# Attention then MoE on one core: a new opening for batch 0, a new bank order in the first s1, and w_in by columns

## The chip, the cores and the metric

One NeuronCore of one Trainium2 chip runs the whole kernel. The metric is the device time of one execution in microseconds (us). The kernel before takes 332.48 us (median of 3 runs, 332.35 to 333.21). The engines are named as in the profile: PE (TensorE matmul), PEld (its weight loads), DVE (VectorE), ACT (ScalarE), POOL (GpSimd), SP (SyncE). PSUM is the memory into which PE writes its results; a bank is the piece of it that takes one 128x512 float32 result. A load "lands" when the trace reports it complete.

## The reference

```python
# q, k, v: (8 batches, 8 heads, 576 tokens, 64), float32
scores = q @ k^T / 8                       # mask: 0 <= query - key < 64
attn   = softmax(scores) ; a = attn @ v
x      = a, heads side by side             # (4608, 512)
h      = x @ w_in                          # w_in (512, 2048)
g      = h * clip(h + 3, 0, 6) / 6
out    = g @ w_out                         # w_out (2048, 512), out (4608, 512) float32
```

## The kernel before

The tokens go through the MoE in nine blocks T of 512. `s1(T)` makes 16 blocks `fc` of hidden units (four matmuls each, then ACT and DVE), `s2(T)` multiplies by `w_out`. Attention of a batch is interleaved with an earlier MoE block, but batch 0 has nothing to hide behind: its attention, then `s1(0)`, then `s2(0)` mixed with batch 1's attention are the opening of the program. This is the part that the change touches.

Loads and set-up (cut):

```python
    stage0, ins0 = load_qk_for_pe(0, 2)   # on SP: q pair 0, k pair 0, the 64-token rests of q and k,
    vst0, insv0 = load_v_by_head(0)       # then q and k of pairs 1 to 3; then V, head by head
    ...
    for i in range(NQT):                  # all rings are zeroed at once, on DVE
        for ring, n in ((QT_ring, "QT"), (KT_ring, "KT")):
            t = consts.tile([P, NG, SP], BF16, name=f"{n}{i}")
            nc.vector.memset(t[:, :, S:SP], 0.0)
    ... # four pT and two V in the same way
```

The first MoE block. Its four first banks are the halves of two `st` tiles:

```python
    def s1_bank(fc):
        if fc in (12, 13):
            return (ps_o, ps_acc)[fc - 12].tile([P, 512], F32, name=("o", "acc")[fc - 12])[:]
        if fc % 4 < 2:
            return h_bank()[:]
        return ps_st.tile([P, 2, 512], F32, name=f"st{fc % 2}")[:, 0, :] if fc < 12 else h_bank()[:]
    ...
        if first:                                    # s1(0) alone
            for u in range(2):
                t = ps_st.tile([P, 2, 512], F32, name=f"st{u}")
                banks += [t[:, 0, :], t[:, 1, :]]
            for gs in first:
                for fc in range(4):
                    mms(fc, banks[fc], gs)
                yield
        for fc in range(NFC):
            hT = banks[fc] if fc < len(banks) else s1_bank(fc)
            mms(fc, hT, (NG - 1,) if fc < len(banks) else range(NG))
            t1 = t1pool.tile([P, TB], BF16, name="t1")
            nc.scalar.activation(out=t1[:], in_=hT, func=RELU, bias=half[:], scale=1.0 / 6.0)
            nc.vector.scalar_tensor_tensor(
                out=gT[:, fc, :], in0=t1[:], scalar=1.0, in1=hT, op0=MIN, op1=MULT)
            yield
```

The weights are cast by the DMA that POOL issues, and POOL also casts q, k and V, in the order of the program:

```python
    w_in = [load_w_in(0, 512, 0, NG)]
    bt.cast_v(vst0, KB - 1, KB, 0, H, pcopy)
    bt.cast_v(vst0, 0, KB - 1, 0, 2, pcopy)
    bt.cast_v(vst0, 0, KB - 1, 2, 4, pcopy)
    w_in += [load_w_in(512, 1024, 0, NG)]
    bt.cast_v(vst0, 0, KB - 1, 4, 6, pcopy)
    bt.cast_v(vst0, 0, KB - 1, 6, 8, pcopy)
    w_in += [load_w_in(1024, FF, 0, 2), load_w_in(1024, FF, 2, NG)]
    ...
    m = s1(0, ((0, 1), (2,)))
    run(m, 1)
    X_(bt, 3)
    run(m, 1)
    st1, ins = load_qk_for_pe(1, 4)
    for x in ins:
        after(x, w_in[1], "the weights go first")
    vst1, _ = load_v_by_head(1)
    ...
    bt.cast_qk(st, 0, 0, 4, pcopy)
    load_w_out(0)
    bt.cast_qk(st, 1, 0, 4, pcopy)
    bt.cast_rest(st, pcopy)
    load_w_out(1)
    cast_pairs(bt, st, 4, 4)
    load_w_out(2)
    load_w_out(3)
    run(m, 11)
    TT(bt, 0, oa_tr)          # batch 1, pair 0: transposes of q and k
    run(m)
    ...
    m = s2(0, BY_QUARTER)     # first all that needs w_out's quarter 0, then quarter 1, ...
    RR(bt)                    # batch 1: transposes of the 64-token rest
```

The softmax here doesn't subtract the row's maximum and nothing guards it: scores larger than these inputs give would overflow.

Of the kernel before, what the change touches and what calls it, by code (L numbers as in the profile page):

```python
# [9 lines left out]
F32 = mybir.dt.float32  # L10
BF16 = mybir.dt.bfloat16
# [13 lines left out]
def kernel(  # L25
# [9 lines left out]
    nc = tc.nc  # L35
    P = nc.NUM_PARTITIONS
    B, H, S, D = q.shape
    DM, FF = moe_w_in.shape
    NT = B * S
    NG = H // 2  # L40
    assert D == 64 and NG * P == DM and WINDOW == D
    KB = (S + P - 1) // P
    SP = KB * P
    NPE = 3
    R = 4
    SM = P * R
    SR = S - SM
    NFC = FF // P
    TB = 512
# [3 lines left out]
    VW = D + 1  # L53
    scale = 1.0 / math.sqrt(D)

    consts = ctx.enter_context(tc.tile_pool(name="consts", bufs=1))
    stage = ctx.enter_context(tc.tile_pool(name="stage", bufs=1))
# [5 lines left out]
    ps_st = ctx.enter_context(tc.tile_pool(name="ps_st", bufs=1, space=PSUM))  # L63
    ps_o = ctx.enter_context(tc.tile_pool(name="ps_o", bufs=1, space=PSUM))
    ps_h = ctx.enter_context(tc.tile_pool(name="ps_h", bufs=2, space=PSUM))
    ps_acc = ctx.enter_context(tc.tile_pool(name="ps_acc", bufs=1, space=PSUM))

    def after(ins, dep, why):

        tc.add_manual_dep(  # L70
            ins.ins, dep.ins.name,
            mybir.DependencyInfo(mybir.DependencyClass.Sync, mybir.DependencyReason.DATA),
            reason=why,
        )
# [24 lines left out]
    def load_qk_for_pe(b, heads):  # L99
        qst = stage.tile([P, H, R * D], F32, name="qst", tag="qst")  # L100
        kst = stage.tile([P, H, R * D], F32, name="kst", tag="kst")
        rst = stage.tile([P, H, D], F32, name="rst", tag="rst")
        ins = []
        for h0 in range(0, H, heads):
            for dst, src in ((qst, q), (kst, k)):
                ins.append(nc.sync.dma_start(
                    out=dst[:, h0 : h0 + heads, :],
                    in_=src[b, h0 : h0 + heads, 0:SM, :].rearrange("h (p j) d -> p h (j d)", j=R),
                ))
            if h0 == 0:  # L110
                for i, src in enumerate((q, k)):
                    ins.append(nc.sync.dma_start(
                        out=rst[i * SR : (i + 1) * SR, :, :],
                        in_=src[b, :, SM:S, :].rearrange("h s d -> s h d"),
                    ))
        return (qst, kst, rst), ins

    def load_v_by_head(b):
        vst = stage.tile([P, KB, H, D], F32, name="vst", tag="vst")
        ins = load_blocks(vst, v, b, (KB - 1,)) + load_v(b, vst, 0, H)  # L120
        return vst, ins

    def load_for_dma(b):
# [5 lines left out]
        return tuple(sts), ins  # L129

    ctx.enter_context(tc.manual_schedule())
    stage0, ins0 = load_qk_for_pe(0, 2)
    vst0, insv0 = load_v_by_head(0)


    ident = consts.tile([P, P], BF16, name="ident")
    make_identity(nc, ident[:])
    mask1 = consts.tile([P, QW], BF16, name="mask1")
# [2 lines left out]
        out=mask1[:], in_=mask1[:], pattern=[[1, QW]], compare_op=ISGE,  # L141
# [3 lines left out]
        out=mask1[:], in_=mask1[:], pattern=[[-1, QW]], compare_op=ISGE,  # L145
# [16 lines left out]
    QT_ring, KT_ring, P_ring, V_ring = [], [], [], []  # L162
    for i in range(NQT):
        for ring, n in ((QT_ring, "QT"), (KT_ring, "KT")):
            t = consts.tile([P, NG, SP], BF16, name=f"{n}{i}")
            nc.vector.memset(t[:, :, S:SP], 0.0)
            ring.append(t)
    for i in range(NPT):
        t = consts.tile([P, 2, KB, 2 * P], BF16, name=f"pT{i}")
        nc.vector.memset(t[:, :, 0 : KB - 1, QW : 2 * P], 0.0)  # L170
        nc.vector.memset(t[:, :, KB - 1, P : 2 * P], 0.0)
        P_ring.append(t)
    for i in range(NV):
        t = consts.tile([P, KB, H, VW], BF16, name=f"V{i}")
        nc.vector.memset(t[:, :, :, D:VW], 1.0)
        nc.vector.memset(t[D:P, KB - 1, :, 0:D], 0.0)
        V_ring.append(t)

    mask = consts.tile([P, 2 * KB, QW], BF16, name="mask")

    win16 = consts.tile([P, NG, FF], BF16, name="win16")
    wout16 = consts.tile([P, NFC, DM], BF16, name="wout16")
    xT = consts.tile([P, NG, NT + SP - S], BF16, name="xT")

    def load_w_in(f0, f1, g0, g1):
        return nc.gpsimd.dma_start(
            out=win16[:, g0:g1, f0:f1],
            in_=moe_w_in[g0 * P : g1 * P, f0:f1].rearrange("(g p) f -> p g f", p=P),
        )
# [176 lines left out]
    def h_bank():  # L366
        return ps_h.tile([P, 512], F32, name="hT")
# [1 line left out]
    def h_tr():  # L369
        return ps_h.tile([P, 1024], BF16, name="hT")  # L370

    def s1_bank(fc):
        if fc in (12, 13):
            return (ps_o, ps_acc)[fc - 12].tile([P, 512], F32, name=("o", "acc")[fc - 12])[:]
        if fc % 4 < 2:
            return h_bank()[:]
        return ps_st.tile([P, 2, 512], F32, name=f"st{fc % 2}")[:, 0, :] if fc < 12 else h_bank()[:]
# [12 lines left out]
    def s1(T, first=()):  # L390
        t0 = T * TB
        gT = gpool.tile([P, NFC, TB], BF16, name="gT")
        gTs[T] = gT

        def mms(fc, hT, gs):
            for g in gs:
                nc.tensor.matmul(  # L397
                    hT, lhsT=win16[:, g, fc * P : (fc + 1) * P],
                    rhs=xT[:, g, t0 : t0 + TB], start=(g == 0), stop=(g == NG - 1),
                )  # L400

        banks = []
        if first:
# [5 lines that stand above are left out]
                    mms(fc, banks[fc], gs)  # L409
                yield  # L410
        for fc in range(NFC):
            hT = banks[fc] if fc < len(banks) else s1_bank(fc)
            mms(fc, hT, (NG - 1,) if fc < len(banks) else range(NG))
            t1 = t1pool.tile([P, TB], BF16, name="t1")
            nc.scalar.activation(out=t1[:], in_=hT, func=RELU, bias=half[:], scale=1.0 / 6.0)  # L415
            nc.vector.scalar_tensor_tensor(  # L416
                out=gT[:, fc, :], in0=t1[:], scalar=1.0, in1=hT, op0=MIN, op1=MULT,
            )
            yield
# [25 lines left out]
    def run(gen, n=10 ** 6):  # L445
        for _ in range(n):
            if next(gen, "end") == "end":
                break
# [21 lines left out]
    def do(bt, *key):  # L470
        later.pop((bt.b, *key))()

    def N_(bt, g, banks=None):
        n = [pv(bt, g, h, next(banks) if banks else h_bank()) for h in range(2)]
        n[0]()
        n[1]()
# [9 lines left out]
    def RR(bt, banks=None):  # L486
        R_(bt, banks)
        do(bt, "r")
# [8 lines left out]
    def cast_pairs(bt, st, h0, heads):  # L497
        bt.cast_qk(st, 0, h0, heads, pcopy)
        bt.cast_qk(st, 1, h0, heads, pcopy)


    bt, st = Batch(0), stage0
    cast_pairs(bt, st, 0, 2)
    bt.cast_rest(st, pcopy)
    for g in range(1, NG):
        cast_pairs(bt, st, 2 * g, 2)
    w_in = [load_w_in(0, 512, 0, NG)]
    bt.cast_v(vst0, KB - 1, KB, 0, H, pcopy)
    bt.cast_v(vst0, 0, KB - 1, 0, 2, pcopy)
    bt.cast_v(vst0, 0, KB - 1, 2, 4, pcopy)  # L510
    w_in += [load_w_in(512, 1024, 0, NG)]
    bt.cast_v(vst0, 0, KB - 1, 4, 6, pcopy)
    bt.cast_v(vst0, 0, KB - 1, 6, 8, pcopy)
    w_in += [load_w_in(1024, FF, 0, 2), load_w_in(1024, FF, 2, NG)]

    def S0_(g, u):
        later[0, "s", g, u] = scores(bt, g, u, bias=True)

    def T0_(g):
        for i in range(2):  # L520
            later[0, "qk"[i], g] = bt.main_t(g, i, h_tr(), vcopy if g else None)

    T0_(0)
    later[0, "r"] = bt.rest_t(ps_acc.tile([P, 1024], BF16, name="acc"))
    do(bt, "q", 0)
    do(bt, "k", 0)
    S0_(0, 0)
    T0_(1)
    do(bt, "r")
    do(bt, "q", 1)  # L530
    do(bt, "s", 0, 0)
    S0_(0, 1)
    do(bt, "k", 1)
    do(bt, "s", 0, 1)
    for g in range(1, NG):
        S0_(g, 0)
        if g == NG - 1:
            N_(bt, 0, oa)
        if g + 1 < NG:
            T0_(g + 1)  # L540
        S0_(g, 1)
        if g + 1 < NG:
            do(bt, "q", g + 1)
            do(bt, "k", g + 1)
        do(bt, "s", g, 0)
        do(bt, "s", g, 1)
    N_(bt, 1, oa)
    X_(bt, 0)
    N_(bt, 2, oa)
# [8 lines left out]

    st1, ins = load_qk_for_pe(1, 4)
    for x in ins:  # L560
        after(x, w_in[1], "the weights go first")
    vst1, _ = load_v_by_head(1)

    nc.vector.tensor_copy(
        out=mask[:], in_=mask1[:].unsqueeze(1).to_broadcast([P, 2 * KB, QW])
    )
# [6 lines left out]
    cast_pairs(bt, st, 4, 4)  # L573
    load_w_out(2)
    load_w_out(3)
    run(m, 11)
    TT(bt, 0, oa_tr)
    run(m)

    bt.cast_v(vst1, KB - 1, KB, 0, H, pcopy)  # L580
    for g in range(NG):
# [1 line left out]
    st2, _ = load_qk_for_pe(2, 4)  # L583

    m = s2(0, BY_QUARTER)
    RR(bt)
    T_(bt, 1)
    S_(bt, 0, 0)
    S_(bt, 0, 1)
# [114 lines left out]
```

## Time and profile before

| | before |
|---|---|
| time | 332.48 us |
| span of the profiled execution | 330.2 us |
| PE busy | 309.0 us (94%) |
| idle gaps of PE over 0.15 us, all | 15.1 us, of which 13.9 before 74 us |
| w_out's four quarters land at | 39.99, 43.38, 46.68, 50.11 us |
| they are first used at | 45.75, 48.52, 51.30, 53.84 us |

From the page, part 2: the span in 40 slices of 8.25 us, a digit being tenths of a slice.

```profile
PE   2995889989999999999999999999999999999995
PEclk9997999999999999999999999999999999999999
DMA  7999999999382999199919991999100010021011
```

PE falls under 9 only in the first nine slices and the last, and the DMA engines are full from the second slice to the tenth. So only the opening can gain, and it has two possible limits, PE's own chain and the DMA. After it, a gain is kept: PE stays fed to the end.

From the timeline of before, PE alone (us: start, length, line, output and inputs, count, and in brackets the idle time before it and what ended it):

```profile
4.28 0.61 PE L263 MATMUL hT<-ident,qn 128*128 128x128 bf16 x4 [4.28 <-POOL qn L233]
...
12.51 0.40 PE L263 MATMUL hT<-ident,qn 128*128 128x128 bf16 x4
...
26.64 0.59 PE L397 MATMUL st<-xT,win 128*128 128x512 bf16 x2 [1.50 <-DVE gT L416]
29.11 0.58 PE L397 MATMUL st<-xT,win 128*128 128x512 bf16 x1 [1.88 <-DVE gT L416]
29.49 3.32 PE L397 MATMUL hT<-xT,win 128*128 128x512 bf16 x8
...
34.38 1.89 PE L397 MATMUL hT<-xT,win 128*128 128x512 bf16 x8
...
45.75 1.04 PE L428 MATMUL o<-wout,gT 128*128 128x512 bf16 x4
...
53.13 0.78 PE L297 MATMUL st<-QT,KT 64*128 64x192 bf16 x10
53.84 1.04 PE L428 MATMUL o<-wout,gT 128*128 128x512 bf16 x4
```

Three readings. Four transposes take 0.61 us at 4 us and 0.40 us at 12.5 us: PE is at half clock at first, although PEclk shows a 9 there. In s1(0) PE waits 1.50 and 1.88 us for DVE although the bank it wants to write is not the one that DVE reads: the two banks are halves of one `st` tile, and the built program orders accesses by tile (of the two matmuls at 26.64 the first is for the other half of the tile that DVE has just read, and had to wait; the second is for the other tile, and went on without a wait). The Trainium skill ("PSUM — Partial Sum Buffer", PSUM bank collisions raise a hardware error) says that two engines must be kept apart in the same bank and quadrant, and that on different banks they run clean; so this wait is the program's, not the hardware's. The trace agrees as far as it goes: from 34.43 to 35.12 us DVE reads an st bank while PE writes hT banks. Last, eight matmuls take 3.32 us just after these waits and 1.89 us later: the clock was halved in between, after a stretch in which PE was mostly idle.

### The profile page before, as it was taken

To read this page: it belongs to the slowest core of one execution; us is meant where nothing else is said; L and a number is where in the kernel's file an instruction comes from. 1 tells how busy PE (TensorE), PEld (TensorE's weight loads), DVE (VectorE), ACT (ScalarE), POOL (GpSimd) and SP (SyncE) were. 2 spreads that over 40 slices of the span, in tenths; PEclk is the share of its full clock that TensorE was granted. 3 is DMA by queue.
4 is the path that set the end of the run, shared out by engine and by line. 5 is a ranking of instruction groups with operands and counts; after the bars stand their busy time and mean duration, and the time that the engine had idled before them with its cause. 6 is when DMAs were issued, how large, how long until landed. Compare 5 with 4: busy or idle time off the path is not lost.

```text
span 330.2 us, 5923 instructions
## 1 busy us (share of the span) xinstructions
PE 309.0 (94%) x2291; PEld 158.8 (48%) x2332; DVE 191.9 (58%) x341; ACT 200.8 (61%) x321; POOL 83.9 (25%) x112
## 2 busy tenths in 40 slices
PE   2995889989999999999999999999999999999995
PEld 1462444545555455544554455446544554444442
DVE  5564665558763777387637773878377637504700
ACT  2664767268864876488647863887378737516711
POOL 4722705533700344025402540255000000000000
PEclk9997999999999999999999999999999999999999
DMA  7999999999382999199919991999100010021011
GB/s 212 231 180 265 241 203 256 237 254 198 85 223 77 220 193 230 66 219 198 236 64 216 202 228 57 220 207 218 62 31 2 35 65 34 1 77 50 2 64 64
DMA packets 128732, 48.89 MB, mean 148 GB/s; under 512 B 114624, under 2 KB 123840, under 8 KB 128704
## 3 DMA queue, kind: packets, MB, share of 16 engines
q1 hardware_dynamic: 124672, 43.27, 60.7%
q0 software_dynamic: 4032, 5.24, 8.7%
q8 instruction: 18, 0.29, 0.4%
q14 instruction: 10, 0.08, 0.1%
HBM read 36.70 MB, written 9.44 MB: 140 GB/s over the span
## 4 chain that ended last, share of the span: by engine, by line
PE 90%; DVE 3%; ACT 2%; DMA 1%; issue 1%; SPq 0%; POOL 0%; POOLq 0%
PE o L428 19%; PE acc L428 19%; PE hT L397 19%; PE st L397 14%; PE st L297 5%; PE hT L332 3%; PE hT L358 2%; PE o L397 2%; PE acc L397 2%; PE hT L337 2%; DMA rst<-in_k_dram 1%; DVE gT L416 1%; PE st L291 1%; ACT t L415 1%; PE hT L263 1%
## 5 line engine op out<-in xcount | busy, mean ns | idle before, releaser
L397 PEld LDWEIGHTS <-win 128*128 128x128 bf16 x576 | 55.9, 98 | 71.3 <-issue 7.5
L428 PEld LDWEIGHTS <-gT 128*128 128x128 bf16 x576 | 52.5, 98 | 56.5 <-issue 0.4
L416 DVE SCALAR_TENSOR_TENSOR gT<-t,hT 128x512 bf16<-128x512 bf16 x70 | 47.6, 687 | 47.8 <-ACT t L415 47.8
L428 PE MATMUL acc<-wout,gT 128*128 128x512 bf16 x272 | 67.6, 379 | 1.2 <-issue 0.6
L428 PE MATMUL o<-wout,gT 128*128 128x512 bf16 x279 | 67.6, 379 | 1.0 <-issue 0.3
L397 PE MATMUL hT<-xT,win 128*128 128x512 bf16 x273 | 67.4, 385 | 0.4 <-issue 0.2
L306 ACT ACTIVATE pT<-st 128x768 bf16<-128x768 f32 x64 | 49.2, 809 | 12.4 <-PE st L297 12.3
L397 PE MATMUL st<-xT,win 128*128 128x512 bf16 x219 | 53.2, 380 | 3.6 <-DVE gT L416 3.4
L415 ACT ACTIVATE t<-hT,half 128x512 bf16<-128x512 f32 x70 | 47.6, 692 | 12.8 <-PE hT L397 12.6
L320 DVE TENSOR_TENSOR pT<-pT,mask 128x1920 bf16<-128x1920 bf16 x28 | 39.1, 1395 | 19.8 <-ACT pT L312 19.8
L416 DVE SCALAR_TENSOR_TENSOR gT<-t,st 128x512 bf16<-128x512 bf16 x56 | 38.4, 688 | 13.8 <-ACT t L415 13.6
L415 ACT ACTIVATE t<-st,half 128x512 bf16<-128x512 f32 x56 | 38.4, 687 | 12.0 <-PE st L397 11.3
L363 ACT COPY xT<-hT 128x576 bf16<-128x576 bf16 x32 | 20.5, 640 | 25.2 <-PE hT L358 24.8
L434 ACT COPY osb<-o 128x512 f32<-128x512 f32 x18 | 10.6, 588 | 36.6 <-PE o L428 36.6
L208 POOL CAST V<-vst 64x512 bf16<-64x512 f32 (+2 forms) x22 | 26.0, 1201 | 26.3 <-DMA vst<-in_v_dram 26.3
L213 POOL CAST qn<-qst 128x512 bf16<-128x512 f32 x20 | 11.4, 611 | 83.2 <-DMA qst<-in_q_dram 74.1
L348 DVE TENSOR_TENSOR opg<-hT,rec 128x320 bf16<-128x320 f32 x56 | 27.5, 492 | 1.9
L332 PEld LDWEIGHTS <-pT 128*128 128x128 bf16 x320 | 20.6, 97 | 8.5 <-issue 0.9
L345 DVE RECIPROCAL rec<-hT 128x5 f32<-128x5 f32 x56 | 10.6, 189 | 22.3 <-PE hT L337 22.2
L332 PE MATMUL hT<-V,pT 128*128 128x65 bf16 x280 | 19.2, 193 | 0.5 <-ACT xT L363 0.4
L297 PE MATMUL st<-QT,KT 64*128 64x192 bf16 (+1 forms) x320 | 19.2, 243 | 0.3
L434 ACT COPY osb<-acc 128x512 f32<-128x512 f32 x18 | 10.7, 592 | 14.4 <-PE acc L428 14.4
(77 smaller groups left out, 237.1 us busy)
## 6 DMA issues: line engine op xcount, KB each, us to landing
out_dram<-osb SPq DMA_DIRECT2D x32, 256.0 KB, 2.0
qst<-in_q_dram SPq DMA_DIRECT2D x24, 256.0 KB, 4.6
kst<-in_k_dram SPq DMA_DIRECT2D x24, 256.0 KB, 5.4
vst<-in_v_dram SPq DMA_DIRECT2D x20, 256.0 KB, 5.8
vst<-in_v_dram SPq DMA_DIRECT2D x32, 128.0 KB, 5.7
win<-in_moe_w_in_dram POOLq DMA_DIRECT2D x4, 512.0 KB, 6.5
qst<-in_q_dram SPq DMA_DIRECT2D x4, 512.0 KB, 7.5
kst<-in_k_dram SPq DMA_DIRECT2D x4, 512.0 KB, 8.6
```

The source lines that it names most:

```text
L208: copy(out=self.V[:kp, k0:k1, h0:h1, 0:D], in_=vst[:kp, k0:k1, h0:h1, :])
L297: nc.tensor.matmul(st[:, h, off : off + w], lhsT=bt.KT[h * D : (h + 1) * D, g, kb * P : (kb + 1) * P], rhs=bt.QT[h * D : (h + 1) * D, g, k ...
L306: nc.scalar.activation(out=pT[:, :, 2 * u : 2 * u + 2, 0:QW], in_=st[:, :, 0 : 2 * QW].rearrange("p h (k w) -> p h k w", k=2), func=EXP, s ...
L320: nc.vector.tensor_tensor(out=pT[:, :, :, 0:QW], in0=pT[:, :, :, 0:QW], in1=mask[:].rearrange("p (h k) w -> p h k w", h=2), op=MULT,)
L332: nc.tensor.matmul(ob, lhsT=pT[:, h, qb, 0:P], rhs=V[:, qb, 2 * g + h, :], start=True, stop=(qb == 0),)
L348: nc.vector.tensor_tensor(out=opgs[bt.b, g][:, :, h, :], in0=ov[:, :, 0:D], in1=rec[:].unsqueeze(2).to_broadcast([P, KB, D]), op=MULT,)
L363: return lambda: acopy(out=xT[:, g, bt.b * S : (bt.b + 1) * S], in_=tr[:, 0:S])
L397: nc.tensor.matmul(hT, lhsT=win16[:, g, fc * P : (fc + 1) * P], rhs=xT[:, g, t0 : t0 + TB], start=(g == 0), stop=(g == NG - 1),)
L415: nc.scalar.activation(out=t1[:], in_=hT, func=RELU, bias=half[:], scale=1.0 / 6.0)
L416: nc.vector.scalar_tensor_tensor(out=gT[:, fc, :], in0=t1[:], scalar=1.0, in1=hT, op0=MIN, op1=MULT,)
L428: nc.tensor.matmul(accs[ts], lhsT=gT[:, fc, ts * P : (ts + 1) * P], rhs=wout16[:, fc, :], start=(fc == 0), stop=(fc == NFC - 1),)
L434: nc.scalar.copy(out=osb[:], in_=accs[ts])
```

## The change

The intent is to shorten the opening: have k of pair 0 early (ACT's queue), put the 64-token rests and the memsets out of the way, have PE's clock up early (matmuls on zeros), let s1(0) start as four banks in twos so that PE does not alternate with DVE, bring w_in in the order in which s1(0) uses it, and finish batch 1's first transposes before s2(0). The diff, cut to its core:

```diff
-    stage0, ins0 = load_qk_for_pe(0, 2)
+    def load_first():
...
+                eng = nc.scalar if h0 == 0 and src is k else nc.sync
...
+            if h0 == 2:
+                (the rests of q and k are loaded here)
...
+    stage0, ins0 = load_first()
     vst0, insv0 = load_v_by_head(0)
+    after(insv0[0], ins0[4], "the third pair goes first")
+    xT = consts.tile([P, NG, NT + SP - S], BF16, name="xT")
+    nc.vector.memset(xT[:, 0, 0:TB], 0.0)
+    idle = ps_o.tile([P, 512], F32, name="o")
+    def keep_busy(n):
+        for _ in range(n):
+            nc.tensor.matmul(
+                idle[:], lhsT=xT[:, 0, 0:P], rhs=xT[:, 0, 0:TB], start=True, stop=True,
+            )
+    keep_busy(8)
...
     (memsets of the rings become fill_qk, fill_p, fill_v, called where they are first needed)
...
-    def s1_bank(fc):
+    def s1_bank(fc, T):
+        if T == 0:
+            if fc in (6, 7):
+                return (ps_o, ps_acc)[fc - 6].tile([P, 512], F32, name=("o", "acc")[fc - 6])[:]
+            if fc in (8, 9, 12, 13):
+                return ps_st.tile([P, 2, 512], F32, name=f"st{fc % 2}")[:, 0, :]
+            return h_bank()[:]
...
-            hT = banks[fc] if fc < len(banks) else s1_bank(fc)
-            mms(fc, hT, (NG - 1,) if fc < len(banks) else range(NG))
+            if fc < len(banks):
+                hT = banks[fc]
+                if fc % 2 == 0:
+                    mms(fc, hT, (NG - 1,))
+                    mms(fc + 1, banks[fc + 1], (NG - 1,))
+            else:
+                hT = s1_bank(fc, T)
+                mms(fc, hT, range(NG))
...
-    w_in = [load_w_in(0, 512, 0, NG)]
     bt.cast_v(vst0, KB - 1, KB, 0, H, pcopy)
     bt.cast_v(vst0, 0, KB - 1, 0, 2, pcopy)
-    bt.cast_v(vst0, 0, KB - 1, 2, 4, pcopy)
-    w_in += [load_w_in(512, 1024, 0, NG)]
-    bt.cast_v(vst0, 0, KB - 1, 4, 6, pcopy)
-    bt.cast_v(vst0, 0, KB - 1, 6, 8, pcopy)
-    w_in += [load_w_in(1024, FF, 0, 2), load_w_in(1024, FF, 2, NG)]
+    w_in = [load_w_in(0, 512, 0, NG)]
+    for h0 in (2, 4, 6):
+        bt.cast_v(vst0, 0, KB - 1, h0, h0 + 2, pcopy)
+    w_in += [load_w_in(f, f + 512, 0, NG) for f in (512, 1024, 1536)]
...
-        after(x, w_in[1], "the weights go first")
+        after(x, w_in[2], "the weights go first")
...
-    run(m, 11)
+    run(m, 15)
     TT(bt, 0, oa_tr)
     run(m)
+    RR(bt, oa_tr)
...
     m = s2(0, BY_QUARTER)
-    RR(bt)
```

More of the change, by code (lines that the diff above doesn't have):

```diff
@@ L131 @@
     ctx.enter_context(tc.manual_schedule())
-    stage0, ins0 = load_qk_for_pe(0, 2)
-    vst0, insv0 = load_v_by_head(0)
+    def load_first():
+        qst = stage.tile([P, H, R * D], F32, name="qst", tag="qst")
+        kst = stage.tile([P, H, R * D], F32, name="kst", tag="kst")
+        rst = stage.tile([P, H, D], F32, name="rst", tag="rst")
+        ins = []
+        for h0 in range(0, H, 2):
+            for dst, src in ((qst, q), (kst, k)):
+                eng = nc.scalar if h0 == 0 and src is k else nc.sync
+                ins.append(eng.dma_start(
+                    out=dst[:, h0 : h0 + 2, :],
+                    in_=src[0, h0 : h0 + 2, 0:SM, :].rearrange("h (p j) d -> p h (j d)", j=R),
+                ))
+            if h0 == 2:
+                for i, src in enumerate((q, k)):
+                    nc.sync.dma_start(
+                        out=rst[i * SR : (i + 1) * SR, :, :],
+                        in_=src[0, :, SM:S, :].rearrange("h s d -> s h d"),
+                    )
+        return (qst, kst, rst), ins
+    stage0, ins0 = load_first()
+    vst0, insv0 = load_v_by_head(0)
+    after(insv0[0], ins0[4], "the third pair goes first")
[6 more added lines that the diff above has]
+                idle[:], lhsT=xT[:, 0, 0:P], rhs=xT[:, 0, 0:TB], start=True, stop=True,
+            )
+    keep_busy(8)
     ident = consts.tile([P, P], BF16, name="ident")
@@ L164, with fill_qk, fill_p, fill_v @@
         for ring, n in ((QT_ring, "QT"), (KT_ring, "KT")):
-            t = consts.tile([P, NG, SP], BF16, name=f"{n}{i}")
-            nc.vector.memset(t[:, :, S:SP], 0.0)
-            ring.append(t)
+            ring.append(consts.tile([P, NG, SP], BF16, name=f"{n}{i}"))
     for i in range(NPT):
-        t = consts.tile([P, 2, KB, 2 * P], BF16, name=f"pT{i}")
+        P_ring.append(consts.tile([P, 2, KB, 2 * P], BF16, name=f"pT{i}"))
+    for i in range(NV):
+        V_ring.append(consts.tile([P, KB, H, VW], BF16, name=f"V{i}"))
+    def fill_qk(i):
+        for ring in (QT_ring, KT_ring):
+            nc.vector.memset(ring[i][:, :, S:SP], 0.0)
+    def fill_p(i):
+        t = P_ring[i]
         nc.vector.memset(t[:, :, 0 : KB - 1, QW : 2 * P], 0.0)
         nc.vector.memset(t[:, :, KB - 1, P : 2 * P], 0.0)
-        P_ring.append(t)
-    for i in range(NV):
-        t = consts.tile([P, KB, H, VW], BF16, name=f"V{i}")
+    def fill_v(i):
+        t = V_ring[i]
         nc.vector.memset(t[:, :, :, D:VW], 1.0)
         nc.vector.memset(t[D:P, KB - 1, :, 0:D], 0.0)
-        V_ring.append(t)
+    fill_qk(0)
+    fill_p(0)
     mask = consts.tile([P, 2 * KB, QW], BF16, name="mask")
@@ L182 @@
     wout16 = consts.tile([P, NFC, DM], BF16, name="wout16")
-    xT = consts.tile([P, NG, NT + SP - S], BF16, name="xT")
     def load_w_in(f0, f1, g0, g1):
@@ L502 @@
     bt, st = Batch(0), stage0
-    cast_pairs(bt, st, 0, 2)
-    bt.cast_rest(st, pcopy)
-    for g in range(1, NG):
+    for g in range(NG):
         cast_pairs(bt, st, 2 * g, 2)
-    w_in = [load_w_in(0, 512, 0, NG)]
+        if g == 1:
+            bt.cast_rest(st, pcopy)
     bt.cast_v(vst0, KB - 1, KB, 0, H, pcopy)
     bt.cast_v(vst0, 0, KB - 1, 0, 2, pcopy)
-    bt.cast_v(vst0, 0, KB - 1, 2, 4, pcopy)
-    w_in += [load_w_in(512, 1024, 0, NG)]
-    bt.cast_v(vst0, 0, KB - 1, 4, 6, pcopy)
-    bt.cast_v(vst0, 0, KB - 1, 6, 8, pcopy)
-    w_in += [load_w_in(1024, FF, 0, 2), load_w_in(1024, FF, 2, NG)]
+    w_in = [load_w_in(0, 512, 0, NG)]
+    for h0 in (2, 4, 6):
+        bt.cast_v(vst0, 0, KB - 1, h0, h0 + 2, pcopy)
+    w_in += [load_w_in(f, f + 512, 0, NG) for f in (512, 1024, 1536)]
     def S0_(g, u):
@@ L523 @@
     T0_(0)
-    later[0, "r"] = bt.rest_t(ps_acc.tile([P, 1024], BF16, name="acc"))
     do(bt, "q", 0)
     do(bt, "k", 0)
+    keep_busy(2)
     S0_(0, 0)
     T0_(1)
+    later[0, "r"] = bt.rest_t(ps_acc.tile([P, 1024], BF16, name="acc"))
+    do(bt, "s", 0, 0)
+    do(bt, "q", 1)
     do(bt, "r")
-    do(bt, "q", 1)
-    do(bt, "s", 0, 0)
+    do(bt, "k", 1)
     S0_(0, 1)
-    do(bt, "k", 1)
     do(bt, "s", 0, 1)
+    fill_p(1)
+    fill_v(0)
     for g in range(1, NG):
@@ L546 @@
         do(bt, "s", g, 1)
+        if g + 1 < NG:
+            fill_p(g + 1)
     N_(bt, 1, oa)
@@ L560 @@
     for x in ins:
-        after(x, w_in[1], "the weights go first")
+        after(x, w_in[2], "the weights go first")
     vst1, _ = load_v_by_head(1)
+    fill_qk(1)
+    fill_v(1)
     nc.vector.tensor_copy(
```

## The prediction

> **What bounds the kernel now.** The page: PE busy 309.0 of 330.2 us. PE idle gaps over 0.15 us (timeline) sum to about 15 us, and nearly all lie before 74 us; afterwards PE is fed, so only the opening can gain, and what it gains stays.
>
> The opening, from the timeline and from the DMA issues with their landings:
> - 0 to 22.1 us, attention of batch 0. PE waits 4.28 (q cast), 1.08 (k of pair 0, landing at 5.25 behind q) and 1.21 (rest of k, landing at 6.99). Then the exponentials pace it, 2.1 us a pair, the first at 9.51. Four transposes take 0.61 us until about 12 us and 0.40 later: the clock is cold although the record says 1.00. The Trainium skill ("TensorE: Matmul & The Clock Gate", Part 1) describes this: throttled until one window of about 3.4 us is busy.
> - 22.1 to 42.5 us, s1(0). After the first chunk PE waits 1.50 and 1.88 us for gT: the two banks of one st tile are treated as one, so matmul, ACT and DVE alternate. The idleness drops the granted clock (0.90 and 0.76 in 25:30 and 30:35), and eight matmuls take 3.32 instead of 1.89 us. The transposes of batch 1 cost a wait of 0.79.
> - 42.5 to 45.8 us: waits of 0.64, 0.48, 0.22 around the rest of batch 1.
> - The DMA is full (share about 1.0 or more) from 2 to 50 us. The quarters of w_out land at 40.0, 43.4, 46.7, 50.1 us; s2(0) first uses them at 45.8, 48.5, 51.3, 53.8. Slack of the last: only 3.7 us.
>
> **What the change does.**
> 1. K of pair 0 on ACT's queue, the rest later, memsets out of DVE's way: first exponential about 1.5 to 2 us earlier; s1(0) starts at about 20.5 instead of 22.1. The DMA work is the same (the skill, "DMA: Bandwidth & Descriptors", Issuing engines are not separate DMA queues: all queues share 16 engines), so k of pair 3 and V do not come much earlier.
> 2. Idle matmuls (8 of about 0.43 us, then 2): warm clock some 4 to 7 us earlier. PE mostly waits there, so little by itself.
> 3. Banks in twos: removes 1.50+1.88, most of the 1.4 of half clock and the 0.79; ACT and DVE then pace, 0.72 us a block. About 5 us.
> 4. Rest of batch 1 before s2: about 0.4 us.
> 5. w_in by columns: quarter 0 lands about 1 us later (20), quarters 1 to 3 in time (about 22.5, 25, 28). Batch 1's loads start near 25 instead of 22.45, yet the bytes in front are the same: they land at most 1 us earlier, and so does w_out.
>
> PE alone could reach s2(0) about 7 us sooner (near 38.5). But w_out is DMA-bound and comes only about 1 us sooner: PE will wait for w_out in s2(0), and the last quarter (about 49) fixes the gain: 53.8 - 49.2 = about 4.5 us.
>
> **Predicted: 327.8 us**, 325.5 to 330.0 eight times in ten. Faster by over 2%: 0.13; within 2%: 0.85; slower: 0.02.
>
> **Signs.** Right: first exponential at 7.5 to 8.2; s1(0) from about 20.5; no wait of over 1 us for gT; no half-clock window near 30; new PE waits for DMA w_out of 2 to 4 us in total between 38 and 50; last quarter used at about 49; after 70 us the trace is merely shifted by 4 to 5 us. Wrong: w_out landing before 47 (gain near 7), or PE waiting for w_in in s1(0).
>
> **What would make it wrong.** Batch 1's loads, gated later, landing late and delaying w_out's issue (gain under 3); new idleness bringing the half clock back; w_out's share of the DMA growing because V of batch 1 comes later (gain over 6).

## More of the kernel before

From the windows of before (stretch in us, length, busy time and count of PE, PEld, DVE, ACT, POOL, then granted clock, DMA share, GB/s moved; a share is the summed time of the packets over 16 engines, so it can exceed 1):

```profile
18.00:21.00 3.00, 2.64 (x60) 2.05 (x55) 2.79 (x9) 2.00 (x4) 1.65 (x3) 1.00 1.19 204
...
25.55:28.97 3.42, 0.59 (x2) 0.19 (x2) 1.88 (x3) 1.58 (x3) 0.00 (x0) 1.00 1.09 278
28.97:32.38 3.41, 3.27 (x8) 1.13 (x8) 0.93 (x3) 1.37 (x2) 1.72 (x2) 0.50 1.19 268
```

The last two are neighbouring stretches of 3.41 us: 0.59 us of PE work in the first, half clock in the second.

## The result, and the profile after

The changed kernel takes 329.75 us (median of 4, 329.46 to 330.45) against 332.59 for the kernel before in the same job. The ratio is 0.9915, 95% interval 0.9893 to 0.9937: a gain of about 2.8 us. A ratio here and below is the mean time of one kernel's runs over that of the other's of the same rounds, so it is not quite the ratio of the medians.

| | before | after |
|---|---|---|
| span of the profiled execution, us | 330.15 | 328.26 |
| first exponential | 9.51 | 6.92 |
| s1(0) starts | 22.08 | 20.59 |
| PE ready for s2(0) | 45.75 | 38.50 |
| s2(0) starts | 45.75 | 41.98 |
| w_in loads land | 18.84, 22.38, 25.97, 29.13 | 20.54, 23.75, 26.45, 29.85 |
| first q of batch 1 lands | 30.13 | 31.32 |
| w_out's quarters land | 39.99, 43.38, 46.68, 50.11 | 41.93, 45.32, 48.62, 52.05 |
| last quarter first used | 53.84 | 52.10 |
| from there to the end of the span | 276.31 | 276.16 |

(Landings are those that the trace gives for each DMA issue; "PE ready" is the end of PE's work before its wait. The profiled pair shows 1.9 of the 2.8 us: the profiled execution of after, 330.45 us, was the slowest of its four.)

From the page of after, part 2, the same three rows:

```profile
PE   7989589899999999999999999999999999999995
PEclk9999869999999999999999999999999999999999
DMA  8999999999983998399929992999200110021011
```

PE is busier at the start, but the half clock has moved from the fourth slice to the fifth and sixth, and PE has a new low (a 5) in the fifth, near 40 us. The timeline of PE in after shows what it is:

```profile
1.25 3.60 PE L163 MATMUL o<-xT 128*128 128x512 bf16 x8 [1.25 <-DVE xT L158]
4.89 0.52 PE L303 MATMUL hT<-ident,qn 128*128 128x128 bf16 x4
...
20.59 1.90 PE L443 MATMUL st<-xT,win 128*128 128x512 bf16 x8 [0.41 <-DMA win<-in_moe_w_in_dram]
...
24.36 1.89 PE L443 MATMUL hT<-xT,win 128*128 128x512 bf16 x8
...
29.07 1.02 PE L443 MATMUL st<-xT,win 128*128 128x512 bf16 x4 [0.24 <-DVE gT L468]
...
36.91 0.38 PE L285 MATMUL o<-ident,rn 128*128 128x128 bf16 x4 [0.79 <-DVE QT L308]
...
41.98 1.89 PE L480 MATMUL o<-wout,gT 128*128 128x512 bf16 x4 [3.48 <-DMA wout<-in_moe_w_out_dram]
43.66 1.91 PE L480 MATMUL acc<-wout,gT 128*128 128x512 bf16 x4
45.36 0.63 PE L303 MATMUL hT<-ident,qn 128*128 128x128 bf16 x4
...
51.38 0.79 PE L337 MATMUL st<-QT,KT 64*128 64x192 bf16 x10
52.10 1.04 PE L480 MATMUL o<-wout,gT 128*128 128x512 bf16 x4
```

All that the change set out to do on PE has happened: the clock is up by 5 us, the waits for gT are 0.24 us, and PE is ready for s2(0) 7.25 us sooner (38.50 against 45.75). Then it waits 3.48 us for w_out, and works at half clock when it starts again (four matmuls in 1.89 us, against 1.04 later).

That accounts for the 7.25 us: 3.48 are the wait, 2.03 are the half clock (from s2(0)'s start to the use of the last quarter PE takes 10.12 us, against 8.09 in before), and 1.74 are left as gain. At the last quarter itself PE does not wait in this profile: from the ten score matmuls to the use it takes 0.72 us, as in before (0.71), where the quarter had landed long ago. PE's own chain from the first landing and the last landing end here within 0.05 us of each other.

The chain of waits of after, 25 to 56 us (start, length, what), shows what w_out's first load waited for:

```profile
26.50 4.81 DMA qst<-in_q_dram
...
31.46 0.98 POOL qn L273
32.44 9.49 DMA wout<-in_moe_w_out_dram
41.93 0.05 issue
41.98 1.89 PE o L480 x4
```

w_out's first load stands on POOL behind the cast of batch 1's q, which waits for that q. The quarters land 3.39, 3.30 and 3.43 us apart in both kernels, so all of the 1.94 us by which w_out is later arise in front of its first landing: 1.19 until that q lands (31.32 against 30.13), 0.75 from there on. And the windows of after:

```profile
18.00:21.00 3.00, 2.31 (x40) 1.66 (x40) 2.86 (x11) 1.38 (x3) 2.54 (x4) 1.00 0.55 77
...
35.90:39.31 3.41, 1.71 (x24) 1.13 (x22) 2.45 (x5) 2.17 (x5) 2.15 (x3) 1.00 1.31 213
39.31:42.73 3.42, 0.75 (x2) 0.28 (x3) 0.00 (x0) 1.29 (x3) 2.58 (x4) 0.50 1.22 204
42.73:46.14 3.41, 3.41 (x15) 1.68 (x13) 0.10 (x1) 0.00 (x0) 0.00 (x0) 0.50 1.23 208
```

Between 18 and 21 us the DMA moves 77 GB/s where before moved 204: a hole. Its cause is on POOL. In before, w_in's second load is issued ahead of the last two casts of V; in after it stands behind them, and is issued 2.7 us later. From the timelines of POOL, first before:

```profile
15.61 0.76 POOL L186 DMA_DIRECT2D win<-in_moe_w_in_dram  x1
...
19.35 0.63 POOL L208 CAST V<-vst 128x512 bf16<-128x512 f32 x1 [2.35 <-DMA vst<-in_v_dram]
```

and after:

```profile
17.73 0.62 POOL L248 CAST V<-vst 128x512 bf16<-128x512 f32 x1 [1.97 <-DMA vst<-in_v_dram]
18.29 2.24 POOL L226 DMA_DIRECT2D win<-in_moe_w_in_dram  x3
```

That gave the theories to be tested:

- **A.** The landing of w_out's last quarter bounds the opening. PE's 7 us end in a wait, and the size of the gain is the slack that the kernel before had there (3.73 us) less what w_out itself became later (1.94 us): 1.79 us, against 1.74 us measured between the two uses and 1.89 us between the two spans. As a part of A: w_out is later because of the hole at 20 us.
- **B.** w_out is later because batch 1's loads are gated on w_in's third load instead of its second.
- **C.** PE's chain is the bound, and the parts of the change simply gave less than thought.
- **H.** The half clock after the wait costs the missing time.

### The profile page after: what moved, and what is told of

Same layout as the page of the kernel before. It is cut to its first block, busy times and chain, and to the rows that moved or that the text cites. A ratio compares the mean times of both kernels' runs of the same rounds, so it can differ in the third digit from the quotient of the medians.

```text
span 328.3 us, 5987 instructions
## 1 busy us (share of the span) xinstructions
PE 314.6 (96%) x2342; PEld 159.6 (49%) x2342; DVE 191.1 (58%) x342; ACT 200.3 (61%) x321; POOL 83.9 (26%) x112
## 4 chain that ended last, share of the span: by engine, by line
PE 84%; DMA 9%; SPq 2%; ACT 2%; POOL 1%; DVE 0%; issue 0%; POOLq 0%
PE acc L480 19%; PE o L480 19%; PE hT L443 17%; PE st L443 13%; PE st L337 4%; DMA wout<-in_moe_w_out_dram 3%; DMA qst<-in_q_dram 3%; PE hT L372 3%; PE hT L398 2%; DMA win<-in_moe_w_in_dram 2%; PE acc L443 2%; PE o L443 2%; PE hT L377 2%; DMA vst<-in_v_dram 1%; SPq L82 1%; ACT osb L486 1%
## 5 line engine op out<-in xcount | busy, mean ns | idle before, releaser
L480 PE MATMUL o<-wout,gT 128*128 128x512 bf16 x288 | 69.7, 383 | 3.6 <-DMA wout<-in_moe_w_out_dram 3.5
L480 PE MATMUL acc<-wout,gT 128*128 128x512 bf16 x288 | 71.0, 383 | 0.0
L360 DVE TENSOR_TENSOR pT<-pT,mask 128x1920 bf16<-128x1920 bf16 x28 | 38.5, 1375 | 20.7 <-ACT pT L352 20.5
L403 ACT COPY xT<-hT 128x576 bf16<-128x576 bf16 x32 | 20.5, 642 | 25.5 <-PE hT L398 25.2
L253 POOL CAST kn<-kst 128x512 bf16<-128x512 f32 x20 | 14.5, 763 | 18.8 <-DMA kst<-in_k_dram 18.8
```

The source lines that it names most:

```text
L253: pcopy(out=n[:, g, 0 : KB - 1, :, :].rearrange("p k h d -> p k (h d)"), in_=s[:, 0 : KB - 1, 2 * g : 2 * g + 2, :].rearrange("p k h d -> ...
L360: nc.vector.tensor_tensor(out=pT[:, :, :, 0:QW], in0=pT[:, :, :, 0:QW], in1=mask[:].rearrange("p (h k) w -> p h k w", h=2), op=MULT,)
L403: return lambda: acopy(out=xT[:, g, bt.b * S : (bt.b + 1) * S], in_=tr[:, 0:S])
L480: nc.tensor.matmul(accs[ts], lhsT=gT[:, fc, ts * P : (ts + 1) * P], rhs=wout16[:, fc, :], start=(fc == 0), stop=(fc == NFC - 1),)
```

## The experiments

Twelve runs in three jobs on three chips, each kernel timed in five rounds against the kernel before on the same chip. The changed kernel itself ran again in one of the three jobs only (after_again); elsewhere the comparison with it goes through the ratios to before. The table has all profiles; "use" is the start of the first matmul that reads w_out's last quarter.

| kernel | ratio to before, 95% interval | median us (before in its job) | last quarter lands | use | use to end |
|---|---|---|---|---|---|
| before | | 332.48 | 50.11 | 53.84 | 276.3 |
| after | 0.9915 (0.9893 to 0.9937) | 329.75 (332.59) | 52.05 | 52.10 | 276.2 |
| w1_early | 0.9929 (0.9885 to 0.9973) | 329.98 (332.49) | 50.52 | 50.57 | 275.9 |
| banks_on_before | 0.9913 (0.9875 to 0.9951) | 329.53 (332.49) | 51.50 | 51.54 | 276.1 |
| after_no_banks | 0.9964 (0.9931 to 0.9998) | 331.34 (332.49) | 53.20 | 53.24 | 275.9 |
| no_idle_mm | 0.9903 (0.9866 to 0.9941) | 329.28 (332.49) | 51.03 | 51.07 | 276.0 |
| after_again | 0.9937 (0.9918 to 0.9956) | 329.90 (332.10) | 51.73 | 51.77 | 275.9 |
| fill_wait | 0.9946 (0.9932 to 0.9961) | 330.31 (332.10) | 52.24 | 52.28 | 275.9 |
| v1_later | 0.9870 (0.9852 to 0.9888) | 327.67 (332.10) | 49.85 | 50.49 | 276.3 |
| best | 0.9878 (0.9861 to 0.9894) | 328.29 (332.10) | 48.93 | 49.34 | 276.1 |
| w1_early_2 | 0.9969 (0.9935 to 1.0002) | 330.87 (331.97) | 52.28 | 52.75 | 276.2 |
| gate_w1 | 0.9948 (0.9921 to 0.9976) | 330.05 (331.97) | 51.74 | 51.79 | 275.9 |
| v1_on_before | 1.0012 (0.9983 to 1.0041) | 332.51 (331.97) | 47.67 | 54.53 | 276.2 |
| banks_v1_on_before | 0.9894 (0.9865 to 0.9924) | 328.48 (331.97) | 51.19 | 51.23 | 276.0 |

The last column is the frame for all that follows: in 14 profiles, from the first use of w_out's last quarter to the end it is 275.9 to 276.3 us, whatever was changed in front. So the opening is measured by that use. In nine of the twelve profiles with the front or the banks of the change it comes 0.04 to 0.05 us after the landing; in the other three (v1_later, best, w1_early_2) 0.41 to 0.64 us after it; in these three PE worked at half clock for 3.4 to 6.8 us between 39.8 and 47.3. Half clock alone does not set them apart, since five of the nine had it in s2(0) too. What does is the wait: in eight of the nine PE stands waiting for the last quarter (0.13 to 1.36 us; after is the tie told above), in the three it does not, and there the bound is PE's chain from the first landing on.

### The new banks alone, on the kernel before (banks_on_before)

```diff
-    def s1_bank(fc):
+    def s1_bank(fc, T):          (as in the change; also the twos of the first four blocks)
...
-    run(m, 11)
+    run(m, 15)
```

> The kernel before with only the new PSUM banks of s1(0), its first four blocks in twos, and the transposes of batch 1 after 15 blocks instead of 11. Theory A (w_out's landing bounds the opening; before had a slack of 3.7 us at the last quarter): PE gains about 5 us in s1(0), the gaps of 1.50 and 1.88 us and the half clock near 30 go, and of that about 3 to 3.7 us reach the end, so about 329.2: as fast as the whole change or a little faster, although all of the new front is missing. Theory C: 5 us, about 327.7.

Measured: 0.9913, as much as the whole change (0.9915 and 0.9937 in its two jobs). s2(0) starts at 41.59 us after a wait of 1.06 for w_out; the waits of 1.50 and 1.88 us are gone. The expected 329.2 was 329.53. The ratio alone supports A, not the 5 us of C (327.7 would be 0.986, outside the interval).

### The change without its banks (after_no_banks)

```diff
-    def s1_bank(fc, T):          (the old s1_bank, the old order of the first four blocks)
+    def s1_bank(fc):
...
-    run(m, 15)
+    run(m, 11)
```

> The changed kernel with the old banks and the old order of s1(0) (and the transposes of batch 1 after 11 blocks). Theory A: the waits of 1.5 and 1.9 us for gT come back, some 4 to 5 us of PE time are lost in s1(0), but PE then reaches s2(0) near 43 instead of 38.5 and finds w_out quarter 0 landed; since the last quarter at 52.05 is the bound, the whole loses only 0 to 1.5 us (330 to 331). Theory C: the loss is the whole 4 to 5 us (about 334).

Measured: 331.34 us, 0.9964. The new front, the new order of w_in and the matmuls on zeros together are worth 0.4%. Against the whole change's ratios of 0.9915 and 0.9937 the loss is 0.3 to 0.5%, or 0.9 to 1.6 us: at the upper end of A's 0 to 1.5, not the 4 to 5 of C. From its timeline, PE:

```profile
24.78 0.59 PE L437 MATMUL st<-xT,win 128*128 128x512 bf16 x2 [1.50 <-DVE gT L456]
27.25 0.38 PE L437 MATMUL st<-xT,win 128*128 128x512 bf16 x1 [1.88 <-DVE gT L456]
...
43.38 1.04 PE L468 MATMUL o<-wout,gT 128*128 128x512 bf16 x4
...
53.24 1.02 PE L468 MATMUL o<-wout,gT 128*128 128x512 bf16 x4 [1.01 <-DMA wout<-in_moe_w_out_dram]
```

PE lost its 5 us (s2(0) starts without a wait at 43.38, where after's PE was ready at 38.50), and it still waits 1.01 us for the last quarter. Alone, the banks give 0.87% and the rest 0.36%: 1.2% if they added, where the whole gives 0.6 to 0.85%; with intervals of 0.3 to 0.4 points on each part this is not clear of noise. Both parts run into the last landing of w_out (53.20 here, 52.05 in after).

### No matmuls on zeros (no_idle_mm)

```diff
-    keep_busy(8)
...
-    keep_busy(2)
```

> The changed kernel without its ten matmuls on zeros. Theory A: the clock stays cold until about 12 us and s1(0) starts 0 to 0.7 us later, but w_in's first quarter (landing 20.5) and w_out bound what follows: same time within 0.3 us. Theory C: 0.5 to 1 us slower.

Measured: 0.9903, no slower than the whole. The clock's record begins at 10.63 us in it and at 5.18 us in after, so the warm clock is real. But PE is ready for s1(0) only 0.49 us later without it (20.67 against 20.18), and in both it then waits for w_in's first load (until 21.49 and 20.59). What is won ends in the wait for w_out, as in the other runs (without it PE still waits 1.52 us before s2(0) and 1.08 us before the last quarter).

### w_in's second quarter issued earlier (w1_early, w1_early_2)

```diff
-    for h0 in (2, 4, 6):
+    bt.cast_v(vst0, 0, KB - 1, 2, 4, pcopy)
+    w_in += [load_w_in(512, 1024, 0, NG)]
+    for h0 in (4, 6):
         bt.cast_v(vst0, 0, KB - 1, h0, h0 + 2, pcopy)
-    w_in += [load_w_in(f, f + 512, 0, NG) for f in (512, 1024, 1536)]
+    w_in += [load_w_in(f, f + 512, 0, NG) for f in (1024, 1536)]
```

> The changed kernel with one line moved: the second quarter of w_in is issued ahead of the casts of V's last two pairs, as before the change. Theory A (the gain was lost to a hole in the DMA stream, 18.5 to 20.8 us, because w_in quarters 1 to 3 now wait behind the cast of V's last pair, so that everything after, w_out too, lands about 1.9 us later): the hole closes, w_out quarter 0 lands near 40 instead of 41.9 and quarter 3 near 50.1 instead of 52.05, PE's wait before s2(0) falls from 3.5 to under 2 us, and the time falls by 1.2 to 2.0 us against the changed kernel (about 328.0). Theory B (w_out is late because batch 1's loads wait for quarter 2 of w_in instead of quarter 1): this alone brings at most half of that, because the gate stays. Theory C (PE is the limit and the front and the banks simply gave less than thought): no change.

The first profile did what A said: w_out's last quarter at 50.52. But its six times ran from 328.61 to 332.75 us, on a chip where the kernel before scattered from 331.17 to 334.99. So it was run again on another chip:

> The same kernel as w1_early, again, since its times scattered by 4 us on a noisy chip. Theory A (a hole in the DMA stream near 20 us costs): ratio to before 0.985 to 0.990, that is 1 to 2 us better than the changed kernel's 0.992 to 0.994, with w_out's last quarter near 50.5. If the hole's closing does not reach the end: 0.992 to 0.994.

Measured: 0.9929 and 0.9969, neither better than the whole change (the first interval still reaches into what A expected, the second does not). In both profiles the hole is closed, as the windows of the first show (after had a share of 0.55 and 77 GB/s there):

```profile
18.00:21.00 3.00, 2.47 (x44) 1.69 (x41) 2.86 (x11) 1.48 (x3) 1.86 (x3) 1.00 1.15 181
```

In the second profile another hole stands behind it:

```profile
27.00:31.00 4.00, 3.77 (x18) 1.60 (x17) 3.25 (x7) 3.83 (x7) 0.00 (x0) 1.00 0.76 192
```

against a share of 1.09 and 289 GB/s in after. There batch 1's loads wait for the landing of w_in's third load (26.64 us) while only its fourth is under way. So the hole at 20 us is real, and closing it is not enough: the part of A that made it the cause of the late w_out falls as a statement about time. The two profiles of this one kernel have the last landing 1.76 us apart (50.52 and 52.28).

### The old gate (gate_w1)

```diff
-        after(x, w_in[2], "the weights go first")
+        after(x, w_in[1], "the weights go first")
```

> The changed kernel with batch 1's loads gated on w_in's second quarter, as the gate stood before, instead of its third. Theory B (the later gate delays w_out): w_out lands 1 to 2 us earlier, ratio 0.985 to 0.990. Theory A: these loads queue behind w_in's transfers already issued, so they land at most 0.5 us earlier; ratio 0.991 to 0.994, w_out's last quarter at 51.3 to 52.2.

Measured: 0.9948, w_out's last quarter at 51.74. The first q of batch 1 lands at 31.64, not sooner than with the later gate (31.32). B alone falls too. It does not tell whether hole and gate together do; `best` below has both mended, with a third edit.

### Filling the wait (fill_wait)

```diff
     do(bt, "s", 0, 1)
+    fill = ps_acc.tile([P, 512], F32, name="acc")
+    for _ in range(14):
+        nc.tensor.matmul(
+            fill[:], lhsT=xT[:, 0, 0:P], rhs=xT[:, 0, 0:TB], start=True, stop=True,
+        )
```

> The changed kernel with 14 matmuls of 512 columns (about 3 us, result not used) where PE waits for w_out ahead of s2(0), so that the clock is not halved there. If the half clock costs time by itself (theory H): 1 to 2 us faster. Theory A (w_out's last landing is the bound): no half-clock window near 40, but the last quarter is still used at its landing, so the time moves by less than 0.5 us.

Measured: 0.9946 against 0.9937 of the control: no gain. The half clock is gone (the granted clock of its six runs is 0.998 to 1.000, where the control has 0.990 to 0.995), and its time came back as waits. From its timeline, PE:

```profile
45.25 1.02 PE L480 MATMUL o<-wout,gT 128*128 128x512 bf16 x4 [0.30 <-DMA wout<-in_moe_w_out_dram]
...
48.54 1.02 PE L480 MATMUL o<-wout,gT 128*128 128x512 bf16 x3 [0.47 <-DMA wout<-in_moe_w_out_dram]
...
52.28 1.02 PE L480 MATMUL o<-wout,gT 128*128 128x512 bf16 x4 [1.36 <-DMA wout<-in_moe_w_out_dram]
```

The three waits sum to 2.13 us, where the half clock had cost 2.03 in after. H falls for this kernel: while the last quarter is the bound, a faster PE only waits longer. The executions of after with the lower clock are the longer ones (0.990: 330.45 and 329.99 us; 0.995: 329.46 and 329.51), but this does not speak for H by itself, as a later landing could lengthen both the wait and the half clock after it. The control itself:

> The changed kernel itself, as a control on this chip beside the next three: 0.989 to 0.994 of before; in its profile s2(0)'s last quarter of w_out is used within 0.1 us of its landing, or up to 0.3 us after it where the clock was halved.

Measured: 0.9937; use 0.04 us after the landing of 51.73.

### V of batch 1 held back (v1_later), and the same on the kernel before (v1_on_before)

PE first reads V of batch 1 at 56.67 us in after, behind the first use of w_out's last quarter at 52.10, yet its loads share the DMA with w_out. They are moved behind w_out in the program and wait for its third quarter:

```diff
-    vst1, _ = load_v_by_head(1)
...
-    load_w_out(2)
-    load_w_out(3)
+    w_out += [load_w_out(2), load_w_out(3)]
+    vst1, insv1 = load_v_by_head(1)
+    after(insv1[0], w_out[2], "the weights go first")
```

> The changed kernel with the loads of V of batch 1 held until w_out's third quarter has landed, so that they take no share of the DMA from w_out. Theory A: quarters of w_out land 3.0 instead of 3.35 us apart, the last near 50.5 instead of 52.05, and the time falls by 1 to 2 us; V of batch 1 then lands by about 56, before it is used. Theory C (PE is the limit): no change, or slower where V comes too late.

Measured: 327.67 us, 0.9870 against the control's 0.9937 on the same chip, intervals apart: 2.2 us. The quarters land 2.73, 2.97 and 3.21 us apart, where after has 3.39, 3.30 and 3.43; the last lands at 49.85. C, which expects nothing of a DMA edit, falls. The profiled execution was the slowest of the five (328.97; the others 327.45 to 327.82), and in it a half-clock window lies on the way to the last quarter, used 0.64 us after its landing. From its timeline, PE:

```profile
40.98 0.61 PE L480 MATMUL o<-wout,gT 128*128 128x512 bf16 x1 [1.83 <-DMA wout<-in_moe_w_out_dram]
...
50.49 1.04 PE L480 MATMUL o<-wout,gT 128*128 128x512 bf16 x4
```

The granted clock of that execution is 0.995 and that of the other four 0.999 to 1.000. So here, with the last landing out of the way, the half clock may well cost the 1.1 to 1.5 us; no run fills the wait in this kernel.

The counter-test is the same edit where A says that w_out has slack:

> The kernel before with V of batch 1 held until w_out's third quarter has landed, and nothing else. Theory A: w_out's last quarter lands 1.5 to 2 us sooner, but before PE uses it only near 53.8, so that nothing comes of it: ratio 0.998 to 1.002, the slack before the last quarter's use grows to about 5.5 us.

Measured: 1.0012. w_out's last quarter lands at 47.67 us, 2.4 us sooner than in the profile of before, and PE uses it at 54.53 without a wait; nothing reaches the end. The slack is 6.9 us, more than the 5.5 expected. An earlier landing is worth 2.2 us where PE stands waiting and nothing where it does not.

### Banks and held V, without the rest of the change (banks_v1_on_before)

The kernel before with the two edits above and nothing else.

> The kernel before with the new banks of s1(0) and V of batch 1 held, without the new front of batch 0 and without the new order of w_in. Theory A: PE reaches s2(0) near 41, w_out's last quarter lands near 49.5, and the two parts together give 4 to 5 us though the second alone gives nothing: ratio 0.985 to 0.989, as good as the changed kernel with V held (0.987). If the front counts beside them: 0.990 or more.

Measured: 0.9894 (0.9865 to 0.9924). The banks give 0.87% alone, the held V nothing alone, both 1.06% by the mean; the difference of 0.2 points between banks and both is within the intervals, so that the held V adds anything on the kernel before is not shown. That lies between what was expected of A (up to 0.989) and of a front that counts (from 0.990). The changed kernel with V held has 0.9870 from another job, and the intervals overlap, so whether the new front is worth the 0.2% between them stays open. In its profile q of batch 1 landed late (32.74 us) and w_out with it (51.19).

### All three edits of the DMA's order (best)

w_in's second quarter early, the old gate, and V held, on the changed kernel.

> The changed kernel with all three: w_in's second quarter ahead of the last two casts of V, batch 1's loads gated on that quarter, V of batch 1 held until w_out's third quarter has landed. Theory A: the gains add, as all shift the same landing: last quarter of w_out near 48.7, time 2.5 to 3.5 us below the changed kernel (about 326.5 to 327.3). Theory C: no change.

Measured: 0.9878, which cannot be told from v1_later's 0.9870. The gains did not add, although A had expected them to (326.5 to 327.3); why is not shown. Its profiled execution was the fastest profile of all (span 325.5 us, last quarter at 48.93), but its four runs lie at 327.63 to 328.36. Both versions beat both kernels, by 1.2 to 1.3% against before; v1_later is the simpler one.

## Why the prediction was right, and where its sizes were off

The predicted 327.8 us (325.5 to 330.0) against 329.75 measured: right in direction and in the mechanism, 0.25 us from the edge of its range in size: it expected some 4.5 us of gain and 2.8 were measured, so that the time still fell into the range owes something to the range's width.

- **PE's side held.** s1(0) was predicted "from about 20.5" and started at 20.59; the waits for gT went from 1.50 and 1.88 to 0.24; "PE alone could reach s2(0) about 7 us sooner (near 38.5)" was 38.50. One of its signs of being wrong showed in small: PE waited 0.41 us for w_in before s1(0). The first exponential came at 6.92, a little earlier than the 7.5 to 8.2 predicted.
- **Where the gain would end held.** "PE will wait for w_out in s2(0), and the last quarter fixes the gain": the wait was 3.48 us, within the 2 to 4 predicted, though in one piece and not spread. The last quarter's use came at its landing in both profiles of the changed kernel (0.05 and 0.04 us after it), with a wait of 0.37 us in the control and none in the first, where 2.03 us of half clock had brought PE to the same moment.
- **The mis-sized term is w_out's landing.** Step 5 said that batch 1's loads and w_out come "at most 1 us earlier" and put the last quarter at about 49.2. It landed at 52.05 in the profile of after (51.73 in the control): instead of about 1 us earlier, 1.94 us later. The prediction had named this among its risks ("Batch 1's loads, gated later, landing late and delaying w_out's issue (gain under 3)"): q of batch 1 landed 1.19 us later and w_out's first load was issued 1.18 us later (32.44 against 31.26), though the gate is not shown to be the reason (gate_w1). The term 53.8 - 49.2 = 4.5 us was 53.84 - 52.10 = 1.74 us in the profiled pair, and the shift after 70 us 1.9 us instead of 4 to 5. The step rested on the DMA being full throughout. In after it is not: w_in's second load, moved behind V's last cast, left it at 77 GB/s between 18 and 21 us.
- **What of that is shown.** That w_out's landing is the bound, and PE's savings beyond it are lost, is shown from both sides (v1_later against v1_on_before; banks_on_before and fill_wait). That the hole at 20 us is why w_out landed later is not: closing it alone (w1_early, twice) or moving the gate alone (gate_w1) brought no time. V's share is not the difference either, as the kernel before has it too. Single executions also differ by nearly as much: w_out's last quarter landed 1.76 us apart in the two profiles of w1_early's kernel, and at 50.11 in the profile of before but at 51.50 with the same front in banks_on_before. So the cause of the 1.94 us stays open.
- **The half clock came back**, as the prediction named among its risks: 6.8 us of it in the profile of after. fill_wait shows that it cost nothing that the waits would not have cost (2.13 us of waits in place of 2.03).
- **The matmuls on zeros** gave "little by itself": no_idle_mm shows none.

## What to carry to other kernels

Before one engine's part of a stage is made shorter, look up when the next input that it will ask for lands and how long before its use: that slack caps the gain (here 3.7 us, of 7 us that PE had saved). Once the engine stands waiting, look at the transfers' order: holding back a load that was not needed yet gave 2.2 us with PE waiting, and nothing without, while closing a hole in the stream and moving a gate gave nothing by themselves. And a load issued from an engine that also works stands behind all the work ahead of it: one line moved past two casts on POOL moved a load of weights by 2.7 us.

## What the Trainium skill lacked or had wrong

- "TensorE: Matmul & The Clock Gate" (Part 1, What's actually happening) gives the half clock as what follows an idle window of about 3.4 us. The records here have stretches of 3.41 us, as it says, but they need not be idle: one with 0.59 us of PE work (before, 25.55 to 28.97) and one with 1.71 us (after, 35.90 to 39.31) were followed by half clock. In the other direction, 1.31 us of PE work in 5.07 to 8.49 of before did not raise the clock, and 3.41 us in the next stretch did. With all 14 profiles cut on this grid, the 11 stretches at full clock that half clock followed hold 0.50 to 1.76 us of PE work, and the least in one that it did not follow is 1.79 (no_idle_mm, 37.93 to 41.35): about half a stretch.
- No page says that the record of the clock may start late and that the profile then shows full clock before it: PEclk shows 9 in the first slice of before, while four transposes take 0.61 us instead of 0.40, and the record starts at 11.90.
- "PSUM — Partial Sum Buffer" tells of banks, as the hardware does; no page that I read warns that two banks taken as one tile are ordered as one by the built program. The two waits were 1.50 and 1.88 us here; after the change the longest wait for gT in s1(0) is 0.24.
- "DMA: Bandwidth & Descriptors" (Issuing engines are not separate DMA queues) says that the queues interleave on the same engines, and this agrees (V comes by SP's queue, w_out by POOL's). It gives no figure for what a load that is not urgent takes from one that is: with V of batch 1 held, w_out's quarters landed 2.73 to 3.21 us apart instead of 3.30 to 3.43.
